# Causal attention with two MoE layers on one core: raw q and k loaded by GpSimd, two evictions reordered, weight decoding ended earlier

## The chip, the cores and the metric

The kernel runs on one core of a Trainium2 chip. The metric is the device time of one execution in microseconds (us). The core's engines are TensorE (PE: matmuls, and PEld: the loading of their stationary operand), VectorE (DVE), ScalarE (ACT), GpSimd (POOL) and SyncE (SP). SP does no arithmetic here: it issues DMAs, one after the other, and waits with each until its source is ready and its destination is free. A DMA issued by GpSimd stands in GpSimd's own queue in the same way.

## The reference

Inputs are q, k, v of shape (4, 8, 576, 64) (batch, heads, positions, width), s of shape (4, 8, 576), and two pairs of weights of shapes (512, 2048) and (2048, 512).

```python
scores = q @ k.T / sqrt(64)
cum    = cumsum(maximum(s, 0))
scores = where(causal, -1e9, scores + minimum(-(cum[:, None] - cum[None, :]), 0))
attn   = softmax(scores) @ v                  # (4, 8, 576, 64)
x = attn laid out as 2304 tokens x 512
y = maximum(x @ w_in, 0) ** 2 @ w_out         # first MoE
h = y @ w_in2
out = (h * cos(h)) @ w_out2                   # second MoE
```

## The kernel before, in words

The 2304 tokens are cut into nine blocks of 256 (`k` in the first MoE). Attention makes the tokens in the order of blocks; each block is one or two pieces of the query rows of a batch, and a piece times one of the eight heads is a "head" `n` of the program (96 of them). A head has one or two "jobs", each of at most 128 query rows (160 jobs). Heads 24 to 31, 56 to 63 and 80 to 95 have one job each, the others two.

Numbers are carried in two parts, high and low, and each product is three matmuls (high by high, high by low, low by high). The high part is a cast on ACT, the low part a subtraction on DVE or GpSimd.

`step` is the unit of the first two stages. It does the work of one job of attention and one to three "slots" of the first MoE: a slot is either `g1` (one of 16 slices of the hidden layer for one block, 12 matmuls into `hps`) or `g2` (12 matmuls that add the slice's part to `y0` and `y1`). After `g1`, `gact` makes relu, square and high part `gh` on ACT, and `grest` the low part `gl` on DVE. Every engine runs its instructions in the order in which `step` writes them, and waits for its operands.

What `step` does for a head `n` ahead of its first job: `load_raw(n + 3)` fetches raw q and k from HBM into one of two buffers `raw` (L221, on SP); `load_ext` fetches four rows of bias terms into `k2` (L340, on GpSimd); `prep_high` casts `raw` into `hi` and `k2` (L347, L348, on ACT); `prep_low` subtracts (L355, L358, on DVE), after which that `raw` buffer is free for the head two further on. After the scores (`emit_qk`, L502) DVE adds mask and minimum (L516), ACT takes the exponential (L533), GpSimd clears the padding columns of `p` where the keys are no multiple of 128 (L560, 80 times), DVE writes the scaled high and low parts into `p` (L561, L565), SP transposes them (L571), and PE multiplies with v (`emit_pv`, L602). `evacuate` normalises a pair of heads: L630, L638 and L642 on DVE, the last of which empties `pvs`.

When the last slice of a block is done, `g2` evicts `y0` by ACT and `y1` by DVE to `st`, stores both to HBM and sums their squares. The second MoE reads y back in five blocks `j` of up to 512 tokens (`load_y`), scales it (`power_y`, GpSimd) and splits it (`split_y`: high part L927 on ACT, low part L928 on GpSimd); `first_y` and `last_y` do this for the first and second half of a block.

Weights come packed, and each of 32 tiles per layer is decoded by a clip on ACT (L719), two bit operations on DVE (L725, L729), and, in the second layer, a sum of squares (L762 on ACT, L771 on PE), the scales (L778 to L783 on DVE), a cast (L744, ACT) and a subtraction (L753, DVE). A group of slices shares a scale (`group`, `tables`: L788 to L828). `bits` is the number of tiles that a step decodes. The groups of the second layer are slices 0 to 3, 4 to 8 and 9 to 15, and it makes a pass over all five blocks for each. In the second layer the loop at the end does, per slice, `m2_g1` (L1246), the cosine, `m2_g2` (L1301) two slices later, and after a group's last slice the evictions of `o0` to `o3` (L1316 on ACT, L1318 on DVE), and decodes 0.75 tiles per slice until all 32 are done.

## Time and profile before

| | |
|---|---|
| median of 3 runs | 1001.28 us (999.33 to 1001.86) |
| profiled execution | 998.74 us, of which the span from first to last instruction is 997.0 us |
| PE busy | 961.9 us (96%) |
| DVE busy | 723.6 us (73%) |
| ACT busy | 654.6 us (66%) |
| GpSimd busy | 162.3 us (16%) |
| DMA, mean | 127 GB/s, 126.65 MB in 150711 packets |
| TensorE clock | granted in full throughout (1.000) |

The busy time of PE is the time in which at least one matmul is in flight. Attention and the first MoE fill the span to about 615 us, the second MoE the rest. Where PE isn't the bound, the profile shows idle time ahead of a matmul and names the engine whose instruction ended it.

### The profile page before, as it was taken

Reading aid. Unit: us, or ns where it says so; the run is one execution under the profiler, and the core shown is the slowest. Engines: PE = TensorE matmul, PEld = TensorE weight load, DVE = VectorE, ACT = ScalarE, POOL = GpSimd, SP = SyncE. Lnnn points to the kernel's source line nnn. Section 1 sums busy time; section 2 is a strip of 40 time slices with the busy share of each in tenths; the row PEclk is TensorE's granted clock in tenths of the full one; section 3 lists DMA queues with packets and bytes.
Section 4 is the critical chain, followed back from the end, with each engine's and each line's share of the span. In section 5 each row is a group of like instructions: output and inputs, shape, how many; then the busy total and the mean of one; then the engine's idle time right before and its main releaser. Section 6 shows DMA issues by size and latency. Waiting matters only on the chain.

```text
span 997.0 us, 20518 instructions
## 1 busy us (share of the span) xinstructions
PE 961.9 (96%) x7266; PEld 738.4 (74%) x7266; DVE 723.6 (73%) x1865; ACT 654.6 (66%) x1596; POOL 162.3 (16%) x258
## 2 busy tenths in 40 slices
PE   5999899999999999999999999999999999999998
PEld 4798898899999998999999997444544454444444
DVE  6879788878778897777987267798987545545555
ACT  5789776778778777676776587777865443433433
POOL 2000011111111111111210022430043340001101
PEclk9999999999999999999999999999999999999999
DMA  8955589756897876477898579110000000011001
GB/s 275 296 175 181 145 198 197 163 131 161 178 180 168 182 192 150 118 147 164 189 214 167 194 260 354 62 40 1 1 1 1 0 1 1 3 40 43 27 17 64
DMA packets 150711, 126.65 MB, mean 127 GB/s; under 512 B 108048, under 2 KB 125792, under 8 KB 150608
## 3 DMA queue, kind: packets, MB, share of 16 engines
q1 hardware_dynamic: 146688, 119.05, 46.4%
q0 software_dynamic: 3904, 6.29, 2.4%
q8 instruction: 57, 0.93, 0.4%
q14 instruction: 46, 0.38, 0.1%
q10 hardware_dynamic: 16, 0.01, 0.0%
HBM read 85.25 MB, written 15.81 MB: 101 GB/s over the span
## 4 chain that ended last, share of the span: by engine, by line
PE 81%; DVE 10%; ACT 5%; issue 2%; DMA 2%; SPq 0%; DVEq 0%; ACTq 0%
PE hps L857 19%; PE y L886 18%; PE o L1301 17%; PE hp L1246 17%; PE qkp L502 4%; PE pvs L602 4%; DVE wt L750 1%; DVE st L729 1%; DVE sb L516 1%; DMA raw<-in_qk_dram 1%; PE xps L657 1%; DVE wt L753 1%; PE qkp L493 1%; ACT st L719 1%; ACT sb L533 1%
## 5 line engine op out<-in xcount | busy, mean ns | idle before, releaser
L857 PE MATMUL hps<-xh,wt 128*128 128x256 f32 x1152 | 239.8, 291 | 4.2 <-ACT g L868 4.1
L886 PE MATMUL y<-gh,wt 128*128 128x256 f32 x1152 | 236.7, 289 | 0.0
L857 PEld LDWEIGHTS hps<-xh,wt 128*128 128x128 f32 x1152 | 190.3, 192 | 6.9 <-ACT g L868 5.8
L886 PEld LDWEIGHTS y<-gh,wt 128*128 128x128 f32 x1152 | 188.9, 191 | 1.2
L1246 PE MATMUL hp<-yh,wt 128*128 128x512 f16 (+1 forms) x640 | 185.9, 358 | 0.0
L1301 PE MATMUL o<-wt,gh 128*128 128x512 f16 x576 | 171.3, 379 | 2.0 <-ACT wt L1316 1.9
L886 PE MATMUL y<-gl,wt 128*128 128x256 f32 x576 | 163.0, 283 | 2.7 <-DVE gl L876 2.7
L857 PE MATMUL hps<-xl,wt 128*128 128x256 f32 x576 | 163.6, 284 | 0.9 <-DVE xl L674 0.9
L1246 PEld LDWEIGHTS <-wt 128*128 128x128 f16 x960 | 92.2, 98 | 93.3
L1258 ACT ACTIVATE a<-hp,hsc 128x512 f32<-128x512 f32 (+1 forms) x80 | 51.4, 643 | 118.2 <-PE hp L1246 116.8
L868 ACT ACTIVATE g<-hps 128x256 f32<-128x256 f32 x144 | 54.6, 379 | 106.4 <-PE hps L857 104.8
L1246 PE MATMUL hp<-yl,wt 128*128 128x512 f16 (+1 forms) x320 | 114.4, 358 | 0.0
L886 PEld LDWEIGHTS y<-gl,wt 128*128 128x128 f32 x576 | 110.1, 191 | 3.7 <-DVE gl L876 3.1
L857 PEld LDWEIGHTS hps<-xl,wt 128*128 128x128 f32 x576 | 111.0, 193 | 1.4 <-DVE xl L674 1.1
L1301 PE MATMUL o<-wt,gl 128*128 128x512 f16 x288 | 109.2, 379 | 0.4 <-DVE gl L1288 0.4
L1259 DVE TENSOR_SCALAR kf<-a 128x512 f32<-128x512 f32 (+1 forms) x80 | 33.6, 420 | 103.7 <-ACT a L1258 103.3
L1301 PEld LDWEIGHTS <-gh 128*128 128x128 f16 x576 | 56.2, 98 | 66.7 <-issue 2.4
L533 ACT ACTIVATE sb<-sb,nb 128x128 f32<-128x128 f32 (+8 forms) x160 | 93.7, 586 | 11.8 <-DVE nb L516 11.5
L340 POOL DMA_DIRECT2D k<-ext_d x80 | 40.9, 511 | 336.2 <-ACT g L869 94.9
L516 DVE CUSTOM_DVE_ANT_0 sb<-qkp,mask 128x128 f32<-128x128 f32 (+8 forms) x160 | 72.6, 454 | 12.5 <-PE qkp L493 5.5
L1267 ACT ACTIVATE a<-kf 128x512 f32<-128x512 f32 (+1 forms) x80 | 46.8, 585 | 46.9 <-DVE kf L1260 46.4
L876 DVE TENSOR_TENSOR gl<-g,gh 128x256 fp32r<-128x256 f32 x144 | 60.0, 417 | 21.5 <-PE y L886 10.4
(119 smaller groups left out, 1690.3 us busy)
## 6 DMA issues: line engine op xcount, KB each, us to landing
rw<-in_w_dram SPq DMA_DIRECT2D x64, 512.0 KB
raw<-in_qk_dram SPq DMA_DIRECT2D x32, 352.0 KB
raw<-in_qk_dram SPq DMA_DIRECT2D x16, 384.0 KB
v_d<-vt SPq DMA_DIRECT2D x16, 320.0 KB
raw<-in_qk_dram SPq DMA_DIRECT2D x16, 320.0 KB
vb<-v_d SPq DMA_DIRECT2D x32, 160.0 KB
vr<-in_v_dram POOLq DMA_DIRECT2D x15, 320.0 KB, 4.4
y_d<-yst SPq DMA_DIRECT2D x18, 256.0 KB
```

Source lines behind the costliest of these rows:

```text
L340: nc.gpsimd.dma_start(out=hd[n][1][64:68, BT - nq:BT + nl], in_=ext_d[n, :, BT - nq:BT + nl])
L502: nc.tensor.matmul(p[0:r, 0:cn], m[0:kk, qo:qo + r], m[0:kk, BT + c0:BT + c0 + cn], start=(kk == 128), stop=(kk == 68),)
L516: nc.vector.tensor_tensor_reduce(out=sb[0:r, c0:c0 + cn], in0=p[0:r, 0:cn], in1=mask[0:r, mo + c0:mo + c0 + cn], scale=-0.125, scalar=(3.0 ...
L533: nc.scalar.activation(out=sb[0:r, 0:w], in_=sb[0:r, 0:w], func=ACTF.Exp, scale=-1.0, bias=j["nb"], accum_out=pd[n - h % 2]["z"][0:r, ti, ...
L857: nc.tensor.matmul(hp, w[:, a, c * 128:(c + 1) * 128], (xh, xl)[e][:, c, :], start=(n == 0), stop=(n == 3 * KD - 1),)
L868: nc.scalar.activation(out=g, in_=hp, func=ACTF.Relu)
L876: nc.vector.tensor_tensor(out=gl, in0=g, in1=gh, op=ALU.subtract)
L886: nc.tensor.matmul(yps[k][d // 2][:, d % 2, :], w[:, a, d * 128:(d + 1) * 128], (gh, gl)[e], start=(f == 0 and n == 0 and d % 2 == 0), sto ...
L1246: nc.tensor.matmul(hp, w[:, a, c * 128:(c + 1) * 128], (yh, yl)[e][:, c, :], start=(m == 0), stop=(m == 3 * KD - 1),)
L1258: nc.scalar.activation(out=a, in_=hp, func=ACTF.Copy, scale=sm["hsc"][:, j, f:f + 1], bias=0.25)
L1267: nc.scalar.activation(out=a, in_=kf, func=ACTF.Sin, scale=-6.2831850)
L1301: nc.tensor.matmul(ops[j][a], (gh, gl)[e][:, a * 128:(a + 1) * 128], w[:, x, :], start=(first and m == 0), stop=(last and m == 2),)
```

## The change

Five edits. Raw q and k are issued by GpSimd instead of SP. The eviction of y leaves `g2` and stands behind `evacuate` in the step (and after each further slot). In the last block of the first MoE the tiles to decode are limited to the eight of the first group, and the steps that drain the pipeline behind it decode none (`DR_BITS`). In the second MoE `last_y` stands behind `m2_g2`, hence behind the evictions that it issues.

```diff
-DR_BITS = 1
+DR_BITS = 0
...
         raw = at.tile([128, KQ], F32, tag="raw", bufs=2, name="raw")
-        nc.sync.dma_start(out=raw[:, BT - nq:BT + nl], in_=qk[n, :, BT - nq:BT + nl])
+        nc.gpsimd.dma_start(out=raw[:, BT - nq:BT + nl], in_=qk[n, :, BT - nq:BT + nl])
...
         if f == NF - 1:
+            yout.append((k, yps.pop(k)))
+            xb.pop(k)
+
+    yout = []
+
+    def y_evict():
+        while yout:
+            k, ys = yout.pop(0)
             for a in range(2):
                 st = wp.tile([128, 2, BT], F32, tag="stg", bufs=2, name="yst")
-                (nc.scalar.copy if a == 0 else nc.vector.tensor_copy)(st, yps[k][a])
+                (nc.scalar.copy if a == 0 else nc.vector.tensor_copy)(st, ys[a])
...
         _weave(evacuate())
+        y_evict()
         if not attn:
             rests()
...
         for _ in range(moe - 1):
             act(moe_slot())
+            y_evict()
...
-                bits = int(max(0, i - 1) * B8_BITS) - int(max(0, i - 2) * B8_BITS)
+                bits = min(2 * GROUPS[0][1], int(max(0, i - 1) * B8_BITS)) - int(max(0, i - 2) * B8_BITS)
+                bits = max(0, bits)
...
         if new:
-            if p == 0 and j + 1 < NB2 and f == 1:
-                last_y(j + 1)
             if p == 0 and j + 2 < NB2 and f == 3:
                 first_y(j + 2)
...
         if i >= G2LAG:
             m2_g2(*steps2[i - G2LAG])
+        if new and p == 0 and j + 1 < NB2 and f == 1:
+            last_y(j + 1)
```

GpSimd's queue in the one-job stretch that begins with head 24 (`k` are the bias rows, of heads 27, 28 and 29; `raw` is raw q and k, of heads 29 and 30; `p` is the padding, `vr` a fetch of v; lines with + are new):

```order
 L340 DMA k_2298<-ext_d 4x640
 L560 MEMSET p 64x2x64
+L221 DMA raw<-in_qk_dram 128x640
 L340 DMA k_2376<-ext_d 4x640
 L560 MEMSET p 64x2x64
 L380 DMA vr<-in_v_dram 128x2x320
+L221 DMA raw<-in_qk_dram 128x640
 L340 DMA k_2430<-ext_d 4x640
 L560 MEMSET p 64x2x64
```

A fetch of raw now stands ahead of each fetch of bias rows and of each clearing of padding, and these wait until it has been issued.

DVE where the second block's y (`y_1628`) is evicted, between the preparation of a head and the normalisation of a pair:

```order
 L355 TENSOR_TENSOR hi<-raw,hi 64x192
 L358 TENSOR_TENSOR k_2752<-raw,hi 64x256
-L894 COPY yst<-y_1628 128x512
 L630 SCALAR_TENSOR_TENSOR z<-z,vsc 64x2
 L638 RECIPROCAL z<-z 64x2
 L642 SCALAR_TENSOR_TENSOR xp<-pvs,z 64x128
+L902 COPY yst<-y_1628 128x512
 L516 ISA sb,nb<-qkp,mask 128x128
```

The copy moves behind the three instructions of the normalisation. The same happens for the fifth block; at the other seven no normalisation stands behind the copy, and the order is the old one.

ACT in the second MoE around the first eviction of `o` (L1316), before:

```order
L1281 CAST gh<-a 128x512
L762 ACTIVATE rw,wss<-st 128x512
L744 ACTIVATE wt_10492<-st,wsc 128x512
L744 ACTIVATE wt_10494<-st,wsc 128x512
L927 CAST yh<-yr 128x2x256 x2
L1267 ACTIVATE a<-kf 128x512
L1316 ACTIVATE wt_9803<-o_10345,osc 128x512
L1316 ACTIVATE wt_9939<-o_10347,osc 128x512
```

and of the change, where the lines are nine further on or, for the high part of y, six:

```order
L1290 CAST gh<-a 128x512
L762 ACTIVATE rw,wss<-st 128x512
L1276 ACTIVATE a<-kf 128x512
L1325 ACTIVATE wt_9803<-o_10328,osc 128x512
L1325 ACTIVATE wt_9939<-o_10330,osc 128x512
L933 CAST yh<-yr 128x2x256 x2
```

The two high parts of y move behind the evictions, and the two casts of weights that stood here come later in the program, since four tiles fewer have been decoded by then.

## Rows read from the trace of the kernel before

**Rows 1.** The page: busy time, share of the span and instructions of each engine.
```profile
PE 961.9 (96%) x7266; PEld 738.4 (74%) x7266; DVE 723.6 (73%) x1865; ACT 654.6 (66%) x1596; POOL 162.3 (16%) x258
```

**Rows 2.** Waits of PE for the sums' reader: us in total, times, longest.
```profile
PE stat L771 <- DVE wsm L778: 0.4, 1, 0.4
```

**Rows 3.** Waits of ACT for raw, all: us in total, times, longest.
```profile
ACT hi L347 <- DMA raw<-in_qk_dram: 15.6, 12, 4.6
```

**Rows 4.** Waits of PE from 470 to 545 us.
```profile
PE hps L857 <- ACT g L868: 1.4, 3, 0.7
```

**Rows 5.** Timeline, second block's y: start, us, engine, line, operation, names, shapes [idle before].
```profile
191.65 0.68 DVE L894 COPY yst<-y 128x512 f32<-128x512 f32 x1
...
192.96 0.63 PE L602 MATMUL pvs<-vb,pt 128*64 128x64 f16 x15 [1.41 <-DVE xp L642]
```

**Rows 6.** Timeline, fifth block's y.
```profile
380.75 0.69 DVE L894 COPY yst<-y 128x512 f32<-128x512 f32 x1 [1.62 <-PE y L886]
...
382.07 0.63 PE L602 MATMUL pvs<-vb,pt 128*64 128x64 f16 x15 [1.11 <-DVE xp L642]
```

**Rows 7.** Timeline, the fetch of raw for head 29.
```profile
162.71 0.75 DVE L358 TENSOR_TENSOR k<-raw,hi 64x576 fp32r<-64x576 f32 x1
...
166.74 0.40 SPq L221 DMA_DIRECT2D raw<-in_qk_dram  x1
...
167.75 0.35 PE L502 MATMUL qkp<-hi 128*64 128x288 f32 x1 [0.67 <-DVE hi L355]
...
171.02 0.72 ACT L347 CAST hi<-raw 128x640 fp32r<-128x640 f32 x1 [4.63 <-DMA raw<-in_qk_dram]
...
172.22 0.38 PE L857 MATMUL hps<-xh,wt 128*128 128x256 f32 x1 [1.03 <-ACT g L868]
```

**Rows 8.** Lines 380, 340, 560 on GpSimd: ns least/median/most; DMA to landing.
```profile
L380 POOL DMA_DIRECT2D vr<-in_v_dram x15: 735/754/774, 74.5 to 386.9; - x15
...
DMA to landing us min/median/max: 3.3/4.4/6.4
...
L340 POOL DMA_DIRECT2D k<-ext_d x80: 502/508/729, 75.7 to 528.5; - x80
...
L560 POOL MEMSET p<- x80: 197/223/402, 158.4 to 537.6; 128x128 f16 x48, 64x128 f16 x32
```

**Rows 9.** Timeline, DVE between prep_low and the writing of p, head 28.
```profile
165.35 0.64 DVE L561 TENSOR_SCALAR p<-sb 64x576 f16<-64x576 f32 x1
...
167.73 0.75 DVE L358 TENSOR_TENSOR k<-raw,hi 64x576 fp32r<-64x576 f32 x1
...
169.44 0.45 DVE L561 TENSOR_SCALAR p<-sb 64x576 f16<-64x576 f32 x1
```

**Rows 10.** Busy time by stretch: length, PE, PEld, DVE, ACT, POOL, clock, DMA.
```profile
160.00:180.00 20.00, 17.48 (x165) 15.31 (x164) 17.54 (x48) 14.16 (x40) 4.36 (x11) 1.00 0.84 192
```

**Rows 11.** Timeline, the end of the first MoE.
```profile
610.94 0.42 DVE L725 TENSOR_SCALAR st<-st 128x512 int32<-128x512 int32 x1
...
612.00 1.41 DVE L753 SCALAR_TENSOR_TENSOR wt<-st,wsc,wt 128x512 f16<-128x512 f32 x2
...
613.80 0.39 PE L886 MATMUL y<-gl,wt 128*128 128x256 f32 x1 [1.03 <-DVE gl L876]
```

**Rows 12.** Timeline, the first eviction of o.
```profile
642.45 1.32 ACT L744 ACTIVATE wt<-st,wsc 128x512 f16<-128x512 f32 x2
...
643.68 1.12 ACT L927 CAST yh<-yr 128x512 f16<-128x512 f32 x2
...
645.24 1.24 ACT L1316 ACTIVATE wt<-o,osc 128x512 f32<-128x512 f32 x2
...
645.95 0.59 PE L1301 MATMUL o<-wt,gh 128*128 128x512 f16 x2 [1.38 <-ACT wt L1316]
```

**Rows 13.** Timeline, scales and tables of the second group: first and last of ten.
```profile
683.05 0.17 DVE L788 TENSOR_SCALAR win<-wsc 128x5 int32<-128x5 int32 x1
...
684.09 0.20 DVE L828 TENSOR_SCALAR osc<-yin,wil 128x1 f32<-128x1 f32 x1
```

## The prediction

> **What bounds the kernel now.** I began with the page: PE is busy for 961.9 of 997.0 us [rows 1], so the whole that an edit could win is the idle time ahead of matmuls, some 35 us, and not the time in which other engines are busy. Then the waits of PE say who ended that idle time, and the timeline says why that engine was late. The table of stretches shows where to look: in most of them PE is full and nothing outside it matters, while from 160 to 180 us it is busy for 17.48 of 20 us, with DVE at 17.54 and ACT at 14.16 [rows 10]. There, and around 190, 382, 510 to 540 and 600 to 652 us, the waits are single, of 0.4 to 1.4 us, and each has its own cause. So this is a sum of single waits, each of which ends with the instruction that is next latest.

> **y's eviction behind the normalisation.** In the second block DVE copies y1 for 0.68 us from 191.65 and only then normalises; PE, which needs `pvs` emptied, stands idle for 1.41 us [rows 5]. Without the copy in front the normalisation starts 0.68 us earlier, so 0.68 of the 1.41 go. In the fifth block the copy itself waits 1.62 us for the last matmul of y, with the normalisation ready behind it; the whole idle 1.11 us of PE go [rows 6]. The copy is later by the three short instructions; who waits for it is the next `g2`, which comes after a whole `g1` of 12 matmuls, so this costs nothing. Gain 0.68 + 1.11 = **1.8 us**; at least 0.7 (if something else is next latest in the fifth block), at most 2.5 (1.41 + 1.11).

> **Raw by GpSimd.** `prep_low` of head 27 frees the buffer at 162.71 + 0.75 = 163.46 us. SP issues the fetch for head 29 at 166.74, 3.3 us later, since transposes and other DMAs stand ahead of it; the cast on ACT starts at 171.02, 4.3 us after the issue, having waited 4.63 us, and PE then waits 1.03 us for a `g` that was queued behind that cast [rows 7]. In all ACT waits 15.6 us for raw, 12 times [rows 3], nearly all of it where a head has one job. From 470 to 545 us PE waits another 1.4 us for `g` in the same way [rows 4]. So what this can win on PE is 1.03 + 1.4 = **2.4 us**, if raw lands in time.

> Does it? From GpSimd a fetch of v of 320 KB lands 4.4 us after its issue (3.3 to 6.4) and occupies the queue for 754 ns [rows 8]. Raw is 224 to 384 KB, so I take the same 4.4 us, and 0.63 us of queue (half way between the 508 ns of the four bias rows and the 754 ns of v). That is no faster than from SP. What is won is the lag of 3.3 us: the issue can follow `prep_low` at once. For head 29 raw would land at 163.5 + 4.4 = 167.9, when ACT is ready at 171.02 - 4.63 = 166.4: a wait of 1.5 instead of 4.63 us. Done for each of the 12 in the same way, 3.1 of the 15.6 us remain, which I take as nothing on PE. At least the gain is 0 (landing as the slowest of v, 6.4 us: the 12 waits, and others that then arise, come to about 19 us, an estimate made in the same way). At most it is 3.1 us, if PE's wait of 0.67 us at 167.75 [rows 7], for the preparation of a head on DVE, goes as well.

> The price is paid in GpSimd's queue. There the fetch waits for `prep_low`, and the bias rows and the clearing of `p` stand behind it now; before, they ran ahead of it. In the one-job stretches: `prep_low` ends at 167.73 + 0.75 = 168.48, DVE wants to write p at 169.44, 0.96 us later [rows 9]. GpSimd needs 0.63 + 0.51 + 0.22 = 1.36 us [rows 8] and some gaps before p is cleared, so DVE waits 0.4 to 0.5 us there, a wait that is new. Behind it on DVE stand the low parts of p and of `g`, and for the latter PE waits. The same reckoning for each of the 80 clearings gives 22 that are late, by 9.6 us in all. But from 160 to 180 us DVE is idle for 20 - 17.54 = 2.46 us [rows 10], room for half a microsecond per head; where heads have two jobs there is more. I let a tenth through to PE: **1.0 us**; at least 0, at most 9.6. The bias rows themselves come 2 us later, but are used two steps on, so they cost nothing. SP, relieved of 80 issues, only gets earlier.

> One more thing is seen in the rows: writing p takes DVE 0.64 us instead of 0.45 where GpSimd issues a DMA at the same time [rows 9]. With 80 more issues, most beside other DVE work, that is a few us of DVE in all, part of the room just counted. [...]

> **Fewer tiles decoded at the end of the first MoE.** Four tiles of the second layer move from the last 15 us of the first MoE, and the start of the second, to a later point. At 610.94 us DVE does the two bit operations of such a tile, 0.42 us and its successor up to 612.00, before the subtraction of two tiles and the low part of `g`, for which PE waits 1.03 us [rows 11]. Without them the subtraction can start when its cast is done, some 1.0 us earlier: gain 1.0. PE's wait of 0.4 us for the reader of the sums [rows 2] was for the scales of such a pair: gain 0.4. At 645.95 PE waits 1.38 us for `o` to be evicted; ahead of that eviction ACT cast two such tiles (1.32 us) and two high parts of y (1.12 us) [rows 12]. The casts leave with the tiles, the high parts leave with the **move of last_y**: either alone would nearly do, together the 1.38 us go. Sum of both edits 1.0 + 0.4 + 1.4 = **2.8 us**; at least 1.4 (the last wait alone), and no more than 2.8, since these are the whole waits.

> What follows: decoding goes on at the same rate per slice and ends some five slices later, where DVE and ACT have room. The scales and tables of the second group, ten small instructions from 683.05 to 684.29 us [rows 13], move to the last step of the first pass, near 709 us, where DVE has no gap; a low part made there is used two slices later, which covers them, so I take 0; without that cover 1.2 us. The low parts of y on GpSimd come some 2 us later but are needed three slices on (about 15 us).

> **Sum.** 1.8 + 2.4 - 1.0 + 2.8 = 6.0 us. Against the profiled execution that is 998.74 - 6.0 = 992.7 us; it lies 2.5 us under the median of the runs, 1001.28, so for a median I forecast 1001.28 - 6.0 = **995.3 us**.

> **The rivals.**
> - *GpSimd's queue makes DVE the bound* (slower). The 22 late clearings pass to PE in full, 9.6 us, and since DVE then sets the pace, the earlier raw is worth nothing: 1001.28 - 1.8 - 2.8 + 9.6 = 1006.3 us. For it speaks that DVE is busy for 88% from 160 to 180 us; against it that each clearing is late by half a microsecond only, and that p isn't needed by PE for five jobs. It decides the sign once 4.6 of the 9.6 us pass. Chance 0.10.
> - *The waits are handed on.* PE, released earlier, stands before the next late thing (`g` from ACT, most likely), and half of each gain is lost: 1001.28 - 3.0 = 998.3 us. For it speaks that DVE and ACT are near 80 to 90% busy in these stretches; against it that in the second MoE PE runs for tens of microseconds without a wait right after them. Chance 0.20.
> - *Raw lands no earlier.* [...] For it speaks the spread of 3.3 to 6.4 us, against it the median of 4.4. Chance 0.20.
> - The forecast has the remaining 0.50.

> **How the numbers follow.** Low end: the most of each part, 2.5 + 3.1 + 2.8 = 8.4 us, and the runs' own spread (their lowest is 2.0 us under the median): 1001.28 - 8.4 - 2.0 = 990.9, so 990.5. High end: past the handed-on case, with some of the DVE waits, 1000.5; only the slower rival and the tails lie outside, under 2 in 10. A change under 0.3% (3 us: under 998.3 or over 1004.3) can't be told from none. Faster: nearly all of the forecast (0.47), 0.15 of the raw case, half of the handed-on case (0.09), 0.71 together; slower: most of the first rival, 0.07; the rest, 0.22, is the same.

> **What would show it.** Right: the pairs of waits at 193 and 382 us shrink to 0.7 and nothing; ACT's waits for raw fall from 15.6 to under 6 us; PE's idle before `o` at the first eviction is gone; PE busy stays, and the span shrinks by 5 to 7 us. Wrong: DVE's waits for the clearing of p grow by several us and PE's waits for `gl` with them; or raw's landing from GpSimd is well over 5 us; or new waits for `hps` take the place of the old.

## The result, and the profile after

The changed kernel takes 1007.86 us (median of 7 runs, 1003.68 to 1010.8) beside 999.84 us of the kernel before on the same chip (998.35 to 1001.86): a ratio of 1.0073, 95% interval 1.0049 to 1.0097. It is slower, where 995.3 us was forecast. The execution that was profiled took 1009.29 us; over the seven the mean clock goes from 0.990 to 0.997, and the profile has 0.991.

The page of the changed kernel, its span and busy times, answers to [rows 1]:

```profile
span 1007.5 us, 20461 instructions
...
PE 967.4 (96%) x7266; PEld 744.9 (74%) x7266; DVE 729.6 (72%) x1865; ACT 654.9 (65%) x1596; POOL 210.8 (21%) x338
```

PE has the same 7266 matmuls, yet is busy 5.5 us longer than in [rows 1]. That cannot come from a wait; the same work took longer. Two views say where. First the waits of the changed kernel (us in total, times, longest):

```profile
PE qkp L502 <- DMA k<-ext_d: 8.7, 5, 2.6
...
PE qkp L502 <- DVE k L358: 3.2, 1, 3.2
...
ACT hi L347 <- DMA raw<-in_qk_dram: 11.9, 7, 3.4
DVE p L561 <- POOL p L560: 11.1, 15, 1.0
...
PE hps L857 <- ACT g L868: 1.3, 4, 0.5
PE pvs L602 <- DVE xp L642: 0.7, 1, 0.7
```

The first two lines are new: PE waits 11.9 us, in six waits, in the middle of the scores, for the four bias rows in `k2`. (The second line names L358. That of the head that waits had ended at 352.06 us, before the wait began; the one that ends at 356.46 prepares the next head. The rows landed at 356.35, and the matmul starts 0.14 us behind that, as in the other waits. Two more, of 0.7 and 0.4 us, which the view puts down to L561 and L516, end behind a landing in the same way.) What the change aimed at did shrink: PE's waits for `g` are 1.3 us, against 4.1 us before.

Then the table of stretches (length, busy time of PE, PEld, DVE, ACT, POOL, granted clock, DMA share, GB/s), the first line to be read beside [rows 10]:

```profile
160.00:180.00 20.00, 16.65 (x143) 15.54 (x142) 15.93 (x44) 12.34 (x34) 6.62 (x15) 0.83 0.74 164
340.00:360.00 20.00, 16.76 (x167) 16.09 (x167) 14.72 (x41) 11.69 (x31) 5.79 (x11) 0.95 0.91 169
360.00:380.00 20.00, 19.93 (x189) 18.92 (x190) 16.76 (x49) 15.18 (x42) 5.92 (x13) 0.97 0.67 150
500.00:520.00 20.00, 16.96 (x182) 16.44 (x180) 16.96 (x48) 13.90 (x35) 5.39 (x12) 1.00 0.88 175
520.00:540.00 20.00, 20.00 (x217) 19.71 (x217) 17.47 (x51) 14.07 (x36) 6.25 (x14) 1.00 0.97 220
540.00:560.00 20.00, 17.44 (x164) 17.06 (x164) 10.68 (x33) 8.43 (x22) 0.61 (x3) 0.83 0.82 122
```

The mean clock is under 1.00 in four of these stretches and nowhere else in the attention stage. Its lower level is 0.50, as in each full microsecond from 171 to 177 us. At that level 20 x (0.17 + 0.05 + 0.03 + 0.17) = 8.4 us are lost to the clock's mean, so some 17 us pass at it: from 170.20 to 177.03, 357.93 to 361.35 and 542.25 to 549.08 us. It falls three times: 0.6 us ahead of the end of a wait of 2.4 us, 1.4 us behind one of 3.2, and 0.6 us ahead of the end of one of 2.6. Behind a fourth, of 2.2 us up to 519.95 us, it stays at 1.00. The first of these waits, in the timeline of the changed kernel (start, us, engine, line, operation):

```profile
168.00 0.35 PE L502 MATMUL qkp<-hi 128*64 128x288 f32 x1 [0.20 <-DVE hi L355]
170.78 0.47 PE L502 MATMUL qkp<-k 68*64 68x288 f32 x1 [2.43 <-DMA k<-ext_d]
```

and what the clock costs, in the groups of instructions from 171 to 177 us (above) and, in the second fence, from 177 to 183 us (count | busy, mean ns | idle):

```profile
L886 PE MATMUL y<-gh,wt 128*128 128x256 f32 x8 | 2.7, 415 | 0.0
```

```profile
L886 PE MATMUL y<-gh,wt 128*128 128x256 f32 x8 | 1.7, 294 | 0.0
```

These are the matmuls of the high part of one `g2` behind the wait, and of a later one once the clock is back. They overlap with four matmuls of the low part, so the cost is read from starts: the twelve take 2.56 us from 171.53, and 1.53 us from 178.72.

The loss adds up. One and the same stretch of work, 440 us long before and 454 us after:

```profile
145.00:585.00 440.00, 432.60 (x4295) 416.17 (x4294) 334.44 (x1037) 317.99 (x871) 62.74 (x165) 1.00 0.75 170
```

```profile
145.00:599.00 454.00, 439.51 (x4296) 423.17 (x4294) 334.95 (x1037) 317.81 (x872) 104.85 (x235) 0.98 0.76 165
```

Of the 14.0 us, 6.9 (439.51 - 432.60) are the longer time of the same matmuls, the lower clock, and 7.1 (14.49 - 7.40) are idle time of PE. DVE and ACT do no more than before. Outside this stretch the change gains, as the table of milestones shows: start of the named matmul in each profile, and how much later than before it is.

| us | before | changed | raw on SP again | decode limit alone |
|---|---|---|---|---|
| first `g1`, slice 8 of the second block | 144.7 | +0.0 | +2.5 | +3.7 |
| first `g1` of the ninth block | 561.4 | +13.8 | +1.1 | +3.4 |
| second MoE, first slice | 615.3 | +12.1 | -0.6 | +1.6 |
| its slice 10 | 664.7 | +9.4 | -3.3 | -1.1 |
| its slice 30 | 759.1 | +10.4 | -2.4 | -0.2 |
| end | 997.0 | +10.6 | -2.3 | -0.0 |

(The first line's +2.5 and +3.7 arise in the first 125 us, ahead of everything that the change touches; read each column by its steps.) The end of the first MoE gives 1.7 us back, the first evictions of `o` 2.7, and one later eviction takes 1.0.

**Why the rows come late.** GpSimd's timeline ahead of the wait at 168 us, whose rows (head 28) are the second line:

```profile
164.02 0.57 POOL L221 DMA_DIRECT2D raw<-in_qk_dram  x1 [2.38 <-ACT g L868]
164.58 0.52 POOL L340 DMA_DIRECT2D k<-ext_d  x1
165.09 0.22 POOL L560 MEMSET p<- 64x128 f16 x1
165.23 0.74 POOL L380 DMA_DIRECT2D vr<-in_v_dram  x1
```

Raw is issued at 164.02 us, half a microsecond behind `prep_low`, just as forecast, and SP's lag is gone. But the rows stand behind it, and two things happen to them. They are issued later: head 28's at 164.58 instead of 161.6 us. And they land later, as line 340's DMAs show, before (first fence) and now:

```profile
DMA to landing us min/median/max: 1.8/3.2/5.9
```

```profile
L340 POOL DMA_DIRECT2D k<-ext_d x80: 521/522/812, 75.5 to 537.0; - x80
...
DMA to landing us min/median/max: 1.8/3.8/7.5
```

From each fetch's issue and landing and the first matmul of its head's scores I took, for all 80 heads, the time that was left and the time that was needed. Before, at least 5.0 us lay between issue and use, and 2 of 80 fetches took over 5 us. After, 11 heads had under 4.5 us left (the least 3.4), and 16 fetches took over 5 us. Four heads with the longest waits had 3.4 to 4.6 us left and needed 6.1 to 7.5. Most of these slow landings come just behind that of the raw ahead of them: raw issued at 352.62 lands at 358.66 us, the rows issued at 353.18 at 358.84, though they are 10 KB beside 320. None of the 80 lands before the raw that was issued ahead of it.

### The profile page after: what moved, and what is told of

The parts are those of the page before. It is cut to its first block, busy times and chain, and to the rows that moved or that the text cites. A ratio compares the mean times of both kernels' runs of the same rounds, so it can differ in the third digit from the quotient of the medians.

```text
span 1007.5 us, 20461 instructions
## 1 busy us (share of the span) xinstructions
PE 967.4 (96%) x7266; PEld 744.9 (74%) x7266; DVE 729.6 (72%) x1865; ACT 654.9 (65%) x1596; POOL 210.8 (21%) x338
## 3 DMA queue, kind: packets, MB, share of 16 engines
q0 software_dynamic: 10048, 33.03, 12.2%
## 4 chain that ended last, share of the span: by engine, by line
PE 45%; DMA 2%; DVE 2%; issue 2%; ACT 1%; POOL 0%; DVEq 0%; POOLq 0%; ACTq 0%
PE o L1310 18%; PE hp L1255 18%; PE y L886 4%; PE hps L857 4%; DMA k<-ext_d 2%; PE pvs L602 1%; PE qkp L502 0%; ACT wt L744 0%; DVE wsc L783 0%; DVE st L729 0%; DVE a L1282 0%; POOL raw L221 0%; DVE sb L516 0%; DVE wt L753 0%; DVE p L561 0%
## 5 line engine op out<-in xcount | busy, mean ns | idle before, releaser
L886 PE MATMUL y<-gh,wt 128*128 128x256 f32 x1152 | 239.5, 291 | 0.0
L886 PEld LDWEIGHTS y<-gh,wt 128*128 128x128 f32 x1152 | 191.3, 193 | 1.2
L221 POOL DMA_DIRECT2D raw<-in_qk_dram x80 | 45.5, 568 | 283.2 <-ACT gh L870 79.7
L533 ACT ACTIVATE sb<-sb,nb 128x128 f32<-128x128 f32 (+8 forms) x160 | 93.7, 586 | 11.3 <-DVE nb L516 11.0
L516 DVE CUSTOM_DVE_ANT_0 sb<-qkp,mask 128x128 f32<-128x128 f32 (+8 forms) x160 | 72.7, 454 | 12.5 <-PE qkp L493 6.0
L561 DVE TENSOR_SCALAR p<-sb 128x512 f16<-128x512 f32 (+7 forms) x128 | 47.0, 367 | 42.8 <-ACT sb L533 18.9
```

The source lines that it names most:

```text
L221: nc.gpsimd.dma_start(out=raw[:, BT - nq:BT + nl], in_=qk[n, :, BT - nq:BT + nl])
L516: nc.vector.tensor_tensor_reduce(out=sb[0:r, c0:c0 + cn], in0=p[0:r, 0:cn], in1=mask[0:r, mo + c0:mo + c0 + cn], scale=-0.125, scalar=(3.0 ...
L533: nc.scalar.activation(out=sb[0:r, 0:w], in_=sb[0:r, 0:w], func=ACTF.Exp, scale=-1.0, bias=j["nb"], accum_out=pd[n - h % 2]["z"][0:r, ti, ...
L561: nc.vector.tensor_scalar(out=p[0:r, 0:w], in0=sb[0:r, 0:w], scalar1=PSC, scalar2=None, op0=ALU.mult)
L886: nc.tensor.matmul(yps[k][d // 2][:, d % 2, :], w[:, a, d * 128:(d + 1) * 128], (gh, gl)[e], start=(f == 0 and n == 0 and d % 2 == 0), sto ...
```

## The experiments

**Theory A:** raw in GpSimd's queue makes the bias rows late; PE waits for them, and the clock falls. The other four edits gain. **Rivals:** B, the clearing of `p` behind raw makes DVE late; C, a fetch by GpSimd costs in itself; D, another edit is to blame. Ratios are to the kernel before, on the same chip, with 95% intervals.

**1. Raw by SP again** (all other edits kept).

```diff
-        nc.gpsimd.dma_start(out=raw[...], in_=qk[...])
+        nc.sync.dma_start(out=raw[...], in_=qk[...])
```

> The changed kernel with raw fetched by SP again, the other edits kept. Theory A (in GpSimd's queue the bias rows of the next head stand behind raw's wait for the low parts, PE waits 11 us for scores and the granted clock falls to half for 17 us) gives all of the loss to this edit: no wait of the scores for bias rows, granted clock 1.000, and the gains of the other edits seen in the traces (1.7 at the end of the first MoE, 2.7 at the start of the second, about 1.4 for y's eviction, less 1.0 for the tables) are left: 995 us, ratio to before 0.993 to 0.997. Theory D (another edit, such as the y eviction behind the normalisation, makes the low parts and with them the scores late): 1003 us or more.

Measured: 995.69 us, ratio 0.9947 (0.9933 to 0.9962). The stretch of the same work is 439.0 us long, PE busy for 432.56 of it, clock 1.00:

```profile
147.00:586.00 439.00, 432.56 (x4296) 416.39 (x4295) 334.57 (x1037) 317.31 (x871) 63.28 (x165) 1.00 0.74 171
```

No wait for rows is left. D falls: this edit makes the whole loss, 1007.86 - 995.69 = 12.2 us between the two medians, and the rest of the change gains 0.5%.

**2. Raw by GpSimd alone**, on the kernel before.

> The kernel before with raw fetched by GpSimd and nothing else. Theory A: the same waits of the scores for bias rows (about 9 us in 4 to 6 waits) and a clock at half for 10 to 20 us; 1011 us, ratio 1.009 to 1.014. Theory D: no loss, 997 to 1000 us. Theories B (the clearing of p comes late) and C (a fetch issued by GpSimd costs by itself, by its landing or by what it does to DVE) also expect about 1011 us; they part from A in the next two runs.

Measured: 1010.42 us, 1.0107 (1.0073 to 1.014); PE waits 11.5 us for rows, mean clock 0.991 in its profile. The edit alone suffices.

**3. Raw behind the rows**, in the same queue.

```diff
             heads_ahead(i, (next_, load_ext, 2))
+            heads_ahead(i - 1, (nraw, load_raw, 4))
...
-            heads_ahead(i, (nraw, load_raw, 4))
```

> The changed kernel with two neighbours in GpSimd's queue exchanged: raw stands behind the bias rows of the next head instead of ahead of them, so a fetch of bias rows never waits for the low parts made just before. The same DMAs from the same engine. Theory A: the scores' waits for bias rows fall from 11 us to under 2, the clock stays at 1.000, 994 to 998 us. Theory B: the clearing of p stands behind both fetches as before, 1005 to 1008 us. Theory C: the same number of fetches by GpSimd with the same landing, raw later than now, 1005 to 1009 us.

Measured: 997.95 us, 0.9977 (0.9958 to 0.9995). No wait for rows, though 20 of 80 fetches of rows took over 5 us to land (they still have an earlier raw or a fetch of v ahead of them), for in the median 8.1 us lie between issue and use (7.3 before; the least 3.6). In the same work PE is busy within 1 us of before (432.60), and the clock is 1.00:

```profile
147.00:590.00 443.00, 433.45 (x4295) 416.23 (x4294) 334.10 (x1037) 317.11 (x871) 104.95 (x235) 1.00 0.79 169
```

B and C fall as the cause of the loss: the same DMAs by the same engine, exchanged with a neighbour, cost 10 us less. That it stays 2 us above experiment 1 is raw itself, which now waits for the rows' buffer: ACT waits 16.6 us for it and PE 6.9 us for `g`, 3.3 of them in one wait, while the stretch above has a clock of 1.00:

```profile
PE hps L857 <- ACT g L868: 6.9, 8, 3.3
```

**4. The rows by SP, raw by GpSimd.**

```diff
-        nc.gpsimd.dma_start(out=hd[n][1][64:68, ...], in_=ext_d[...])
+        nc.sync.dma_start(out=hd[n][1][64:68, ...].bitcast(F32), in_=ext_d[...])
```

> The changed kernel with the bias rows fetched by SP and raw by GpSimd, so that neither stands in the other's queue. Theory A: no wait of the scores for bias rows unless SP is late with them (then up to 3 us in all), clock 1.000, 993 to 997 us. Theory B: the clearing of p still stands behind raw's wait, but behind one fetch less, 1002 to 1006 us. Theory C: 1004 to 1008 us.

Measured: 1008.27 us, 1.0073 (1.0053 to 1.0092). A miss: I had thought that a queue without raw is enough. In the timeline of this kernel the rows for head 28 stand behind transposes in SP's queue:

```profile
167.46 0.31 SPq L340 DMA_DIRECT2D k<-ext_d  x1
```

```profile
169.27 0.34 PE L502 MATMUL qkp<-hi 128*64 128x288 f32 x1 [0.48 <-DVE hi L355]
174.99 0.47 PE L502 MATMUL qkp<-k 68*64 68x288 f32 x1 [5.37 <-DVE z L638]
```

They are issued 1.8 us ahead of their use, 33 of the 80 under 4.5 us ahead. (`z` has nothing to do with scores. The low part of this head, L358, had ended at 170.00 us, and the last signal of the rows' landing comes at 174.85: what PE waits for is the rows.) So A holds in another form: not raw as such, but whatever stands ahead of the rows. With five late heads and the clock at 0.992 the time is the same as with raw ahead of them.

**5. Late rows without raw's bytes.** Raw on SP, and in GpSimd's queue two, three or five clearings of unused partitions ahead of each fetch of rows.

```diff
+        for _ in range(2):   # 3, 5
+            nc.gpsimd.memset(hd[n][1][96:128, ...].bitcast(F32), 0.0)
         nc.gpsimd.dma_start(out=hd[n][1][64:68, ...], in_=ext_d[...])
```

> The changed kernel with raw fetched by SP, and two clearings of unused partitions of k2 put ahead of each fetch of the bias rows in GpSimd's queue, so that the rows are issued some 1.5 us later, as behind raw, but have no large fetch ahead of them. It parts two ways in which raw's place could hurt. Theory A1 (the later issue alone is enough): PE waits for rows by 5 to 11 us, granted clock at half for 10 to 20 us, 1002 to 1007 us. Theory A2 (the rows must also land behind raw's bytes, 5.7 to 7.5 us after their issue where PE waited, against a median of 3.2 us before): rows land in 3 to 4 us, PE waits under 3 us in all, clock 1.000, 996 to 998 us.

> As the run with two clearings ahead of the bias rows, with five, so that the latest fetches are issued less than 3 us ahead of their use, later than in the changed kernel (3.4 us at the least there). Theory A1 (lateness of issue is enough): waits for rows over 5 us in all, half clock behind some, 1002 us or more. Theory A2 (landing behind raw's bytes is needed for waits long enough to bring the clock down): rows land in 3.0 to 3.5 us, single waits under 1.5 us, clock 1.000, 997 to 1000 us.

> As the runs with two and five clearings ahead of the bias rows, with three: the rows are issued 3.2 to 3.6 us ahead of their use at the least, as in the changed kernel (3.4), with raw on SP. Taking the changed kernel's margins head by head with the landings of before, the waits come to 0.7 us in all, an estimate; with its own landings to 16.5. Theory A2 (the landing behind raw's bytes is needed): waits for rows under 2 us in all, clock 1.000, 996 to 999 us. Theory A1 (this lateness is enough): 5 us of waits or more and 1003 us or more.

| | least time from issue to use | heads under 4.5 us | landing, median | PE waits for rows | time, ratio |
|---|---|---|---|---|---|
| raw on SP, none | 5.0 us | 0 | 3.2 us | none | 995.69 us, 0.9947 |
| two | 3.9 us | 4 | 3.0 us | none | 997.79 us, 0.9976 (0.9961 to 0.999) |
| three | 3.0 us | 8 | 3.2 us | one, of 0.8 us | 998.12 us, 0.998 (0.9968 to 0.9991) |
| five | 1.1 us | 41 | 2.2 us | 9.9 us in 13 | 1011.23 us, 1.0116 (1.0099 to 1.0134) |
| changed kernel | 3.4 us | 11 | 3.8 us | 11.9 us in 6 | 1007.86 us, 1.0073 |

With three, the margins are about those of the changed kernel, and next to nothing is waited for: this lateness alone isn't the cause. (The one wait is that of head 25, which the view puts down to L563; its rows land 4.2 us behind their issue, with 3.3 us left.) With five it is more than enough; there I had expected A2's 997 to 1000 us and was wrong, since the dose went far past the changed kernel's. Its waits (us in total, times, longest) show DVE late for `p` too, but with three clearings DVE waits 14.2 us for GpSimd there and the kernel loses nothing, so it is the rows that cost:

```profile
DVE p L563 <- POOL k L341: 14.9, 18, 1.5
...
PE qkp L504 <- DMA k<-ext_d: 9.9, 13, 2.1
```

So one rule fits every row of the table: PE waits by what the landing exceeds the time left. In the changed kernel both moved: at the eight heads that waited, the time left fell by 1.2 to 2.8 us and the landing rose by 1.5 to 4.6 us. Head by head, an estimate from the two traces: before's margins and landings give no wait; the changed margins with the old landings 0.7 us in all; the old margins with the changed landings 2.5; both changed 16.5. (PE's eight waits come to 13.0 us: the matmul ahead of the one that reads the rows covers a part of each.)

**6. PE kept at work in the waits.** The changed kernel, with the first matmul of the scores done eight times more in five heads.

```diff
+            for _ in range(8 if n in (28, 58, 89, 90, 94) and ti == k == 0 else 0):
+                nc.tensor.matmul(p[...], hi[...], hi[...], start=True, stop=True)
```

> The changed kernel, raw by GpSimd, with the first matmul of the scores done eight times more into the same place in five heads (28, 58, 89, 90, 94), of which four had the long waits of PE for bias rows; the result is the same. PE works for some 2 us where it stood idle; nothing is waited for less. If the halved clock behind such waits is a cost of its own (17 us at half, some 8 us of matmuls): clock 1.000, 1000 to 1003 us. If the waits alone are the loss and the clock only shows with them: 1007 to 1010 us, the waits a little more than before.

Measured: 1004.13 us, 1.0051 (1.0029 to 1.0073), between the two forecasts and with an interval that overlaps the changed kernel's. In its profile waits of 2.1 and 3.7 us remain behind the added matmuls (heads 28 and 58) and one of 1.8 us stands at head 86, which had none: the waits of these heads were not filled. The mean clock is 0.995, beside 0.991 in the changed kernel's profile. It neither shows nor refutes that the clock is a cost of its own; that rests on the 6.9 us of PE's busy time above.

**7. Raw earlier in SP's queue**, ahead of the fetch of `vb`.

```diff
             heads_ahead(i, (nlow, prep_low, 2))
+            if job(i) and jobs[i][0] >= EARLY:
+                heads_ahead(i, (nraw, load_raw, 4))
```

> The changed kernel with raw on SP, issued right behind the low parts in program order, ahead of the fetches of vb and the stores of v instead of behind them. If raw's lag in SP's queue is what ACT's waits for raw (15.4 us) and PE's for g behind them (1.2 us at 175, 2.2 us at 519) come from: ACT's waits 7 to 12 us, 993 to 995 us. If SP's queue only exchanges what is late (vb, and with it the product with v): 995.5 to 998 us.

Measured: 995.61 us, 0.9954 (0.9937 to 0.9971), as experiment 1. PE's waits for `g` fall to 1.7 us, but ACT's for raw are still 13.9, and PE waits once, 2.1 us, for rows that were issued 6.6 us ahead of use. They were issued at 344.11, behind a fetch of v (320 KB, issued at 342.65) that landed at 351.50 us, and PE went on at 353.12, 1.6 us behind that landing: these rows had a fetch of v ahead of them where those of the changed kernel had raw. No gain that can be measured.

**8. last_y back at its old place**, raw on SP.

> The changed kernel with raw on SP and last_y back at its old place in the step, so the move of last_y alone undone. If either edit alone had nearly removed PE's 1.38 us in front of the first eviction of o, as the prediction took it: 995.7 to 996.3 us, the wait under 0.4 us. If the move was needed: the wait is back by 1 us or more, 996.7 to 997.1 us.

Measured: 994.8 us, 0.9949 (0.9931 to 0.9966), under both forecasts and not to be told from experiment 1. The wait of 1.38 us [rows 12] is gone without the move of `last_y`. The decode limit does it alone.

**9. The decode limit alone**, on the kernel before (`DR_BITS = 0` and the bound on `bits`).

> The kernel before with the decode limit alone (DR_BITS 0 and the bound on bits). The prediction gave the limit 1.4 us, and another 1.4 us to it or to the move of last_y. From the traces of the changed kernel I now expect 1.7 us at the end of the first MoE and 2.7 us at the first two evictions of o, less 1.0 us at the third: 996.8 us, ratio 0.995 to 0.998.

Measured: 997.82 us, 0.9976 (0.9964 to 0.9987). By the milestones above it gains 1.8 us to the start of the second MoE (3.4 to 1.6), 2.7 to slice 10 (1.6 to -1.1), and gives 0.9 back to slice 30, 3.6 in all; the medians, 999.71 and 997.82, show 1.9 of it.

**10. y's eviction alone**, on the kernel before.

> The kernel before with y's eviction behind the normalisation alone. By the prediction 1.8 us (0.7 in the second block, 1.1 in the fifth), by the trace of the changed kernel with raw on SP some 1.6 us: 998.4 to 999 us, ratio 0.998 to 0.999, which so many rounds can hardly tell from none; the trace decides it, by PE's waits near 193 and 382 us.

Measured: 998.47 us, 0.9988 (0.9976 to 0.9999). In its profile PE's wait for `xp` at 195 us is shorter by 0.5 us, and the one at 382 us is not there.

**11. The phase of decoding moved**, on the kernel of experiment 8.

```diff
-QUIET = 3
+QUIET = 4
...
-            goal = min(4 * NF, bits0 + int(max(0, i + 1 - QUIET) * P_BITS))
+            goal = min(4 * NF, bits0 + int(max(0, i + 1 - QUIET) * P_BITS + 0.5))
```

> A try at a version under both kernels: the changed kernel with raw on SP, last_y at its old place, and the decoding of weights in the second MoE started one slice later with its phase moved by half a tile, so that in no slice two casts of decoded tiles stand on ACT right ahead of the eviction of o (before, they do at three of nine such places, in the changed kernel at one). If these two casts (1.32 us) are what PE waits for at the eviction at 716 us (1.4 to 1.6 us), and not the tables that moved there, the wait goes: 993.2 to 994.2 us, 1 to 1.5 us under the same kernel with the old phase. If the tables are the cause: 994.8 us and the wait stays.

Measured: 993.89 us, 0.9939 (0.9923 to 0.9955), the lowest of all and below both kernels. What it removes is seen in the changed kernel's timeline at the third eviction of `o`:

```profile
727.82 1.32 ACT L744 ACTIVATE wt<-st,wsc 128x512 f16<-128x512 f32 x2
729.17 0.63 ACT L1276 ACTIVATE a<-kf 128x512 f32<-128x512 f32 x1
729.70 0.67 ACT L1325 ACTIVATE wt<-o,osc 128x512 f32<-128x512 f32 x1
```

```profile
730.42 0.59 PE L1310 MATMUL o<-wt,gh 128*128 128x512 f16 x2 [1.44 <-ACT wt L1325]
```

Two casts of decoded tiles, 1.32 us, stand ahead of the cosine and the eviction. With the phase moved no such wait is left among PE's waits. Against experiment 8 the median is 0.9 us lower, within the intervals; the trace is what decides it: from slice 10 to slice 30 it takes 93.7 us, that of experiment 8 95.3.

## Why the prediction was wrong

**The step that failed** is in the paragraph on raw: "The bias rows themselves come 2 us later, but are used two steps on, so they cost nothing." The delay was about right (the eight heads that waited lost 1.2 to 2.8 us of their margin), but the cover was not checked in a row. The rows' buffer is free only when the scores of the head two before are done, so even before the change the closest fetch had 5.0 us from issue to use. I also let the rows land as before, while I let raw, 30 times their size, go ahead of them in the same queue; 16 of 80 then took over 5 us. Neither alone costs much (experiments 3 and 5 with three clearings), the two together 7 us of idle time and 7 of slow clock.

**The clock** had no term. [Rows 10] show 1.00, and I took it for granted. Other executions of the kernel before, measured beside the experiments, have mean clocks of 0.995 to 1.000, so the full clock was not certain even there.

**Raw's gain** was right in mechanism. Head 29's raw was forecast to land at 167.9 us and landed at 167.98, and ACT's wait of 4.63 us [rows 7] became 0.77. PE's waits for `g` fell by 2.8 us (forecast 2.4). ACT's waits for raw fell only from 15.6 [rows 3] to 11.9 us, not below 6: raw's landing has about the forecast median (4.0 us, forecast 4.4), but 11 of 80 take over 5 us and one 8.4.

**The price on DVE**, 1.0 us with 9.6 as its bound, was the wrong place to look. DVE's waits for the clearing of `p` rose from 8.4 to 11.1 us and were hidden, as taken; with raw on SP again they are 10.5, so little of the rise is raw's. The slower rival gave 1006.3 us, near the result, by a mechanism that did not occur, so that was luck: PE's new waits are for the rows and not for DVE, which is busy for 15.93 us from 160 to 180 us, less than the 17.54 of [rows 10]. The rival in which raw lands no earlier, 6.4 us after its issue, would have left 1001.28 - 1.8 - 2.8 = 996.7 us; no run shows raw so late in general. Its median landing is 4.0 us, and exchanging two neighbours in the queue (experiment 3, 997.95 us) took the loss away with all fetches left on GpSimd.

**y's eviction** was right: forecast 0.68 of 1.41 us and all of 1.11 us. The wait behind [rows 5] is now

```profile
194.71 0.63 PE L602 MATMUL pvs<-vb,pt 128*64 128x64 f16 x15 [0.67 <-DVE xp L642]
```

and the one of [rows 6] is gone; 1.2 us by the medians of experiment 10, 1.7 by its trace.

**Decoding and last_y**, forecast 2.8 us, gained 4.4 in the trace of the changed kernel (1.7 and 2.7) and lost 1.0 at the third eviction, 3.4 net. The split was off: the move of `last_y` is worth nothing measurable beside the limit (experiment 8). **The tables**, taken at 0 with 1.2 us as a bound, were what I had named for that 1.0 ahead of experiment 1, wrongly: the wait is for the eviction behind two casts of decoded tiles, and moving the decoding's phase, with the tables still late, removes it.

**The chances.** The other four edits were forecast to gain 1.8 + 2.8 = 4.6 us, and with raw on SP they gained 4.7 by the medians (1000.36 to 995.69), though the split between them was off. That 995.7 lies near the 995.3 forecast for all five is chance, since that sum holds another 1.4 us for raw. The range lacked the case in which something small, queued behind the moved fetch, has little time left.

## What to carry to other kernels

When a DMA moves to another queue, list what that queue issues behind it, and for each take from the trace the time from its issue to its first use and the time that it takes to land; here the bias rows (7 to 12 KB), issued behind raw (224 to 384 KB), had 1.2 to 2.8 us less left in the eight heads that waited, and 16 of 80 took over 5 us to land, where 2 had before. Where two such delays add up against one margin, check the sum: here the one alone comes to 0.7 us of waits, the other to 2.5, both together to 16.5, an estimate from the two traces (experiment 5). Price a wait of PE of some microseconds with what the clock may do around it: here 6.9 us of slower matmuls came on top of 7.1 us of idle time.
